# Attention outputs of four chunks in one visit of TensorE, with the state term in 32x32 tiles

## The chip, the cores and the metric

The kernel runs on one core of one Trainium2 chip. The metric is the device time of one execution, in microseconds (us). The core has TensorE (PE, with its weight loads shown apart as PEld), VectorE (DVE), ScalarE (ACT), GpSimd (POOL) and SyncE (SP), whose queue issues nearly all transfers (DMAs) here.

## What is computed

Two blocks, one after the other. The first is a Mamba-2 attention over 4 sequences of 768 tokens with 8 heads, head size 32 and state size 16. In the kernel's chunks of 128 tokens (the reference cuts into chunks of 32, which is the same sum) it reads, for each sequence and head:

```python
cum = np.cumsum(log_a_of_chunk, axis=-1)
M = (C @ B.T) * causal * np.exp(cum[:, None] - cum[None, :])
y = M @ x + (C @ state) * np.exp(cum)[:, None]          # inner term + state term
state = exp(cum[-1]) * state + (B * exp(cum[-1] - cum)[:, None]).T @ x
```

The second takes the 3072 tokens (256 columns, 8 heads of 32) through four expert networks, all of them for every token, weighted by the token's normalised probabilities:

```python
for e in range(4):
    out += p[:, e:e+1] * (np.maximum(x @ w1[e], 0) @ w2[e])   # w1 256x1024, w2 1024x256
```

All data is fp32.

## The kernel before

**Chunks and blocks.** There are 24 chunks of 128 tokens; chunk c belongs to sequence c % 4, so chunks c and c + 4 follow each other in one sequence, and the state that chunk c leaves is read by chunk c + 4. The chunks form five blocks for the expert networks, of 4, 4, 4, 6 and 6 chunks (`Block`, L302). Blocks of four use a Strassen-like scheme of 2x2 products, blocks of six one of 3x3 (L273 to L299). The weights are cut into 16 pieces of 256 columns (`fb`). A unit (L1257 to L1267) is the work of a block on some of these pieces: the first layer of this unit is put between the second layer of the unit before (`put`, L1222).

**The engines' parts.** PE does all products (`product`, L826, matmul at L830: 128x128 weights, 256 columns). ACT copies banks of PSUM to SBUF (`snap`, L839; `visit`, L1085) and back (`seed`, L844). DVE and POOL combine (L857), gate (L865), and add up weights (L919) and results (L1136). SP's queue loads weights (L418, L424, L895), sums of weights stored before (L916, stored at L924), gates (L818) and tokens.

**Attention for a pair of chunks.** While a block runs, the next block's chunks are worked in pairs: `fetch` (L700) loads tokens (`load_tokens`, L391: x, B, and B and C transposed), decays for rows (`load_heads`, L404) and decays for columns (L401). `decays` (L714) makes the decay matrix LT by scans on DVE (L455), the masked C (ctm, L436 on ACT), the decay of the state term (dec, L735 on DVE) and cts = ctm x dec (L738 on POOL). `scores` (L742) is one visit of PE for a pair: C B^T by heads in row tiles of 32x128 (L443) into four banks, which DVE multiplies by LT into MT (`masked`, L600). `outputs` (L759) is another visit for the pair: the state term (L774), then the inner term (`inner`, L468, four column tiles of 128x32 at a time), each chunk into a bank of its own. ACT copies the bank to yT (L790), and its last 16 columns by heads, the new state, to A (`keep_state`, L473). `carry` (L797) makes the state S on DVE: a transpose (L806), the decayed old state added (L808), and M = S spread over 4 column groups with zeros elsewhere (L811 with `qmask`, L524).

**The state term before.** A 128-row operand of C holds 8 heads of 16 state rows, two heads to each 32 rows. The state term runs as two matmuls of 64x64 a chunk; in each, M's zeros keep the two groups of 32 rows apart. In chunks 4 and up with odd number, the rows are held with their halves exchanged (`turned_round`, L346), so that a pair uses all four 64x64 tiles of the array. For that their tokens are loaded in three pieces (L394 to L396) and their decays in two (L407, L408), and the state is kept in two copies (L475, L476).

**What sets the order.** PE's order is a list (`line`) written by the loops from L1257 on. `PAIRS_AT` (L33) tells in which unit of a block which pair of the next block is worked; the score visit stands at place `SC` = 1 of the unit's list and the output visit at place `OUT` = 14 (L1330 to L1345). All other engines are ordered by a planner (`Plan`, L61): each work has a cost in us, the latest time at which PE can do with it (`times`), and buffers out of pools (`homes`, L368: 33 V, 32 W, 8 banks, 4 xb, 2 MT, 2 ctm, 2 cts, ...); the planner walks through time, gives each engine the most urgent work that is ready, and so writes the queues once, when the program is built. On the chip each queue runs in that order. In the built program, each transfer of SP also waits for the landing of the one eight issues before it.

Of the kernel before, what the change touches and what calls it, by code (L numbers as in the profile page):

```python
# [12 lines left out]
P = 128  # L13
# [7 lines left out]
KEEP = 5  # L21
NV, NW = 33, 32
SC, OUT = 1, 14
SLACK, BACK, YIELD = 0.0, 1.0, 6.0
# [3 lines left out]
RATE, MARGIN = 310.0, 4.0  # L28
AFTER = 1
HELD = ("x", "w"), (5, 8), (0, 7)  # L30
LAST = (0, 1), (0, 2), (1, 1), (1, 2), (0, 0), (1, 0)
LATE = (13, 2), (6, 9), (11, 4), (10, 12), (3,), (1, 14), ("x", "w"), (5, 8), (0, 7)
PAIRS_AT = {(3, 2): {0: 0, 1: 1}, (4, 2): {0: 0, 2: 1}, (4, 3): {0: 0, 1: 1, 2: 2},  # L33
            (6, 3): {0: 0, 2: 1, 3: 2}}

# [25 lines left out]
class Plan:  # L61
# [12 lines left out]
    def add(self, on, fn, reads=(), writes=(), part=(), lag=0.0, due=None, reuse=None, two=False,  # L74
            port=True, after=None, kb=0):
        w = Work(on, fn, lag)
        w.two, w.port, w.after, w.kb = two, port, after, kb
# [85 lines left out]
    def run(self, line, at, begin):  # L163
# [18 lines left out]
        while todo:  # L182
            e = min(t, key=lambda e: t[e])
            now = t[e]
            best, soon = None, None
            late = self.late = max(0.0, t["PE"] - line[head].nominal) if head < len(line) else 0.0
            for w in waiting[e]:
# [121 lines left out]
def kernel(  # L309
# [35 lines left out]

    def turned_round(c):  # L346
        return c >= NSEQ and c % 2 == 1

# [16 lines left out]
    def some(n, shape, name, pool=const):  # L365
# [9 lines left out]
        "LT": some(2, [P, NH, P], "LT"),  # L375
        "MT": some(2, [P, NH, P + N], "MT"),
        "ctm": some(2, [HN, NT, P], "ctm"),
        "cts": some(2, [HN, NT, P], "cts"),
        "dec": some(4, [HN, P], "dec"),
        "A": some(4, [P, NT, N], "A"),  # L380
        "S": some(6, [HN, D], "S"),
        "M": some(6, [HN, NQ, D], "M"),
        "gate": some(3, [P, max(b.n for b in blocks), P], "gate"),
# [7 lines left out]
    def load_tokens(c, xb):  # L391
        src = xbc[real(c)]
        if turned_round(c):
            nc.sync.dma_start(out=xb[:, :OBT], in_=src[:, :OBT])  # L394
            nc.sync.dma_start(out=xb[:HALF, OBT:], in_=src[HALF:, OBT:])
            nc.sync.dma_start(out=xb[HALF:, OBT:], in_=src[:HALF, OBT:])  # L396
        else:
            nc.sync.dma_start(out=xb, in_=src)
# [5 lines left out]
    def load_heads(c, ah):  # L404
        src = ac_d[real(c)].unsqueeze(1).to_broadcast([NH, N, P])
        if turned_round(c):
            nc.sync.dma_start(out=ah[:HALF], in_=src[NH // 2:])  # L407
            nc.sync.dma_start(out=ah[HALF:], in_=src[:NH // 2])  # L408
        else:
            nc.sync.dma_start(out=ah, in_=src)  # L410

# [37 lines left out]
    def quarter(c, r):  # L449
        q = r ^ 2 * turned_round(c)  # L450
        return slice(NT * q, NT * q + NT)
# [21 lines left out]
    def keep_state(c, A, y):  # L473
        if c % 2:
            nc.scalar.copy(out=A[:HALF], in_=y[HALF:])  # L475
            nc.scalar.copy(out=A[HALF:], in_=y[:HALF])  # L476
        else:
            nc.scalar.copy(out=A, in_=y)

# [43 lines left out]
    nc.vector.memset(zeros, 0.0)  # L523
    qmask = const.tile([P, NQ, D], FP32)  # L524
    nc.vector.memset(qmask, 0.0)
    for q in range(NQ):
        nc.vector.memset(qmask[32 * q:32 * q + 32, q], 1.0)
    own = const.tile([P, 1], FP32)
# [159 lines left out]

    yT, gates, S, M = {}, {}, {}, {}
    yT[0, 0] = plan.taken("V", NV - 3, now)  # L690
# [9 lines left out]
    def fetch(c):  # L700
        s = st[c]
        if "xb" not in s:
            s["xb"] = value("xb")
            dma(lambda e: load_tokens(c, s["xb"].t), 3 if turned_round(c) else 1, 320,
                part=[s["xb"]])
        if c >= NSEQ:
            s["ah"] = value("ah")
            dma(lambda e: load_heads(c, s["ah"].t), 2 if turned_round(c) else 1, 64,
                part=[s["ah"]])
# [32 lines left out]
    def scores(cs):  # L742
# [5 lines left out]
        for r in (3, 2, 0, 1):  # L748
            for j, c in enumerate(cs):
                s = st[c]  # L750
                dve(.42, lambda e, c=c, r=r, s=s, j=j: masked(
                    c, r, s["MT"].t, s["LT"].t, gs_[r].t, j), reads=[gs_[r], s["LT"]],
                    part=[s["MT"]])

# [4 lines left out]
    def outputs(cs):  # L759
# [4 lines left out]
        reads = [st[c][k] for c in cs for k in ("xb", "MT", "cts") if k in st[c]]  # L764
        reads += [M[c - NSEQ] for c in cs if c >= NSEQ]

        def fn(e):
            vs = {}
            for c in cs:
                vs[c] = v = ys[c].t[:, :NT * (P + N)].rearrange("p (t s) -> p t s", t=NT)  # L770
                for h in range(2) if c >= NSEQ else ():
                    rows = slice(HALF * h, HALF * h + HALF)
                    to = HALF * (1 - h if turned_round(c) else h)
                    nc.tensor.matmul(  # L774
                        out=v[to:to + HALF, :, 0:P],
                        lhsT=M[c - NSEQ].t.rearrange("p q d -> p (q d)")[rows, rows],
                        rhs=st[c]["cts"].t[rows], start=True, stop=False,
                        tile_position=(HALF * h, to), skip_group_check=True)
            for c in cs:
# [3 lines left out]

        pe((.96 if cs[0] >= NSEQ else .75) * len(cs), fn, reads=reads, writes=list(ys.values()))
        for c in cs:
# [6 lines left out]
            if c < NCH - NSEQ:  # L792
                s["A"] = value("A")
                act(.34 if c % 2 else .18, lambda e, c=c, s=s, y=y: keep_state(
                    c, s["A"].t, v(y)[:, :, P:]), reads=[y], part=[s["A"]])

    def carry(c):  # L797
        s = st[c]
        if "A" not in s:
            return  # L800
        S[c], M[c] = value("S"), value("M")
        more = [S[c - NSEQ], s["dec"]] if c >= NSEQ else []

        def fn(e):
            t = S[c].t
            nc.vector.transpose(t, s["A"].t.rearrange("p t n -> p (t n)"))  # L806
            if more:
                nc.vector.scalar_tensor_tensor(  # L808
                    out=t, in0=more[0].t, scalar=more[1].t[:, P - 1:P], in1=t,
                    op0=ALU.mult, op1=ALU.add)  # L810
            nc.vector.tensor_mul(M[c].t, t.unsqueeze(1).to_broadcast([HN, NQ, D]), qmask)  # L811

        dve(.82 if more else .54, fn, two=True, reads=[s["A"], *more], writes=[S[c], M[c]])

# [475 lines left out]
    for u, (k, groups) in enumerate(units):  # L1290
# [38 lines left out]
        if k < len(blocks) - 1:  # L1329
            p = PAIRS_AT[len(of_block), blocks[k + 1].scheme.pairs].get(i)  # L1330
            if p is not None:
                cs = [blocks[k + 1].first + 2 * p + j for j in range(2)]
                for c in cs:
                    fetch(c)
                    decays(c)
                for x, make in ((SC, scores), (OUT, outputs)):
                    mark = len(line)
                    make(cs)
                    at[x] = line[mark:]
                    del line[mark:]  # L1340
                for c in cs:
                    carry(c)
        for x, w in enumerate(merged):
# [56 lines left out]
```

## Time and profile before

| | us |
|---|---|
| median of three runs | 630.37 (629.18 to 632.73) |
| the execution that was profiled | 630.59 |
| its span | 628.8 |
| PE busy / weight loads | 622.6 / 529.3 |
| DVE busy | 526.0 |
| ACT busy | 261.9 |
| POOL busy | 254.3 |
| big matmuls, L830, 2656 records | first at 12.8, last visits of attention at 418 |

A record is half of an fp32 matmul: the hardware runs each as two passes, and the trace shows both. In a line of the view in order of time stand the start, the time from the first start to the last end, engine, line, operation, output and inputs, sizes (rows and columns of the tile, then the moving operand), and the number of records; in brackets the idle time ahead of it and who ended it. In a line of a group stand the busy time, the mean of one in ns, and the idle time ahead. "PEq", "SPq" and the like are the engines' queues. Ends of matmuls are modelled; their starts are used here.

### The profile page before, as it was taken

The numbers are of one execution on the slowest core, as the hardware profiler recorded it, in microseconds if no ns is written. First come the engines' busy times: TensorE is split into PE (matmuls) and PEld (weight loads), VectorE is DVE, ScalarE is ACT, GpSimd is POOL, SyncE is SP. The second block draws the span as 40 slices with busy tenths as digits, with TensorE's granted clock in tenths as the row PEclk, the third lists the DMA queues.
The fourth block names the chain that finished last, engine by engine and source line by source line (L and its number), as shares of the span: only waits on it lengthen the run. The fifth ranks groups of instructions, "written<-read, shape, count | busy, mean of one in ns | idle before, by whom it ended". The sixth has DMA issues, their size and how long they took to land.

```text
span 628.8 us, 10190 instructions
## 1 busy us (share of the span) xinstructions
PE 622.6 (99%) x3363; PEld 529.3 (84%) x3363; DVE 526.0 (84%) x869; ACT 261.9 (42%) x538; POOL 254.3 (40%) x267
## 2 busy tenths in 40 slices
PE   9999999999999999999999999999999999999997
PEld 5787888888888888878888888888888888888886
DVE  7988899899997699988778988978787977768684
ACT  4222642434434353344433336355444235455441
POOL 4153552625534764543666421414045521233130
PEclk9999999999999999999999999999999999999999
DMA  7999795484898965699997827546123333951001
GB/s 206 307 304 346 231 302 197 123 282 126 287 336 298 315 189 164 173 322 334 349 365 244 280 63 250 176 118 199 57 80 94 101 73 80 361 176 47 1 1 51
DMA packets 110932, 125.87 MB, mean 200 GB/s; under 512 B 28692, under 2 KB 76832, under 8 KB 110880
## 3 DMA queue, kind: packets, MB, share of 16 engines
q1 hardware_dynamic: 110500, 124.97, 62.3%
q8 instruction: 27, 0.44, 0.3%
q10 hardware_dynamic: 380, 0.25, 0.1%
q14 instruction: 25, 0.20, 0.1%
HBM read 100.30 MB, written 24.89 MB: 199 GB/s over the span
## 4 chain that ended last, share of the span: by engine, by line
PE 93%; DMA 3%; DVE 2%; ACT 1%; issue 0%; SPq 0%; POOL 0%; ACTq 0%; POOLq 0%; DVEq 0%
PE bank L830 87%; PE bank L468 2%; DMA ab<-acut_d 2%; PE bank L443 2%; DMA w<-in_w_dram 1%; PE bank L774 1%; PE bank L603 1%; PE bank L580 0%; DVE LT L455 0%; DVE v L857 0%; DVE v L865 0%; POOL v L857 0%; DVE MT L600 0%; SPq L418 0%; DVE w L919 0%
## 5 line engine op out<-in xcount | busy, mean ns | idle before, releaser
L830 PE MATMUL bank<-v,w 128*128 128x256 f32 x1864 | 438.9, 380 | 0.0
L830 PEld LDWEIGHTS bank<-v,w 128*128 128x128 f32 x1864 | 352.1, 190 | 53.6 <-issue 4.0
L830 PE MATMUL bank<-Y,w 128*128 128x256 f32 x792 | 203.1, 379 | 1.2 <-ACT v L839 1.2
L857 POOL TENSOR_TENSOR v<-v,v 128x512 f32<-128x512 f32 x71 | 101.0, 1424 | 190.4 <-DVE v L857 84.4
L857 DVE TENSOR_TENSOR v<-v,v 128x512 f32<-128x512 f32 x199 | 162.8, 841 | 17.9 <-ACT v L839 14.5
L830 PEld LDWEIGHTS bank<-Y,w 128*128 128x128 f32 x792 | 150.1, 190 | 22.7 <-ACT v L839 2.0
L865 DVE SCALAR_TENSOR_TENSOR v<-bank,gate 128x512 f32<-128x512 f32 x172 | 116.7, 686 | 41.5 <-PE bank L830 34.2
L1085 ACT COPY v<-bank 128x512 f32<-128x512 f32 x107 | 62.6, 585 | 163.3 <-PE bank L830 161.9
L844 ACT COPY bank<-v 128x512 f32<-128x512 f32 (+1 forms) x192 | 108.1, 578 | 27.3 <-DVE v L857 24.4
L919 POOL TENSOR_TENSOR w<-w,w 128x256 f32<-128x256 f32 x102 | 89.9, 901 | 40.3 <-PE bank L830 29.6
L839 ACT COPY v<-bank 128x512 f32<-128x512 f32 x106 | 61.9, 585 | 100.7 <-PE bank L830 97.7
L455 DVE TENSOR_TENSOR_SCAN LT<-ab,ident 128x512 f32<-128x512 f32 x42 | 54.1, 1306 | 2.6 <-DMA ab<-acut_d 2.6
L857 DVE TENSOR_TENSOR v<-bank,v 128x512 f32<-128x512 f32 x40 | 27.6, 689 | 17.6 <-PE bank L830 16.4
L738 POOL TENSOR_TENSOR cts<-ctm,dec 128x256 f32<-128x256 f32 x20 | 19.1, 965 | 43.5 <-DVE dec L735 20.8
L1136 POOL TENSOR_TENSOR v<-v,v 128x256 f32<-128x256 f32 x20 | 17.1, 865 | 45.2 <-ACT v L1085 45.1
L600 DVE TENSOR_TENSOR MT<-bank,LT 128x256 f32<-128x256 f32 x93 | 32.1, 414 | 0.3
L436 ACT ACTIVATE ctm<-xb,tmask 128x128 f32<-128x128 f32 x48 | 15.9, 392 | 27.8 <-DMA w<-in_w_dram 9.8
L1136 DVE TENSOR_TENSOR v<-v,v 128x256 f32<-128x256 f32 x40 | 18.6, 493 | 4.6 <-ACT v L1085 4.3
L461 POOL TENSOR_TENSOR MT<-xb,LT 128x128 f32<-128x128 f32 x20 | 11.1, 566 | 21.9 <-DVE LT L455 20.7
L919 DVE TENSOR_TENSOR w<-w,w 128x256 f32<-128x256 f32 x36 | 17.4, 506 | 0.2
L990 DVE TENSOR_TENSOR bank<-bank,v 128x512 f32<-128x512 f32 x22 | 15.2, 691 | 2.6 <-PE bank L830 2.6
L919 POOL TENSOR_TENSOR w<-w 128x256 f32<-128x256 f32 x13 | 10.2, 790 | 17.4 <-DMA w<-in_w_dram 15.8
(76 smaller groups left out, 216.3 us busy)
## 6 DMA issues: line engine op xcount, KB each, us to landing
w<-in_w_dram SPq DMA_DIRECT2D x130, 256.0 KB
w<-w_d SPq DMA_DIRECT2D x130, 256.0 KB
w_d<-w SPq DMA_DIRECT2D x82, 256.0 KB
ab<-acut_d SPq DMA_DIRECT2D x21, 512.0 KB
w<-in_w_dram SPq DMA_DIRECT2D x38, 128.0 KB
xb<-in_xbc_dram SPq DMA_DIRECT2D x12, 320.0 KB
gate<-p_d SPq DMA_DIRECT2D x10, 384.0 KB
gate<-p_d SPq DMA_DIRECT2D x11, 256.0 KB
```

The lines of the kernel that those rows point to most:

```text
L436: nc.scalar.mul(ctm[:, t], xb[:, OCT:OCT + P], tmask[:, t:t + 1])
L455: nc.vector.tensor_tensor_scan(out=LT.rearrange("p h s -> p (h s)")[:, lo:lo + w], data0=src, data1=ident.rearrange("p h s -> p (h s)")[:, ...
L600: nc.vector.tensor_mul(MT[:, h, 0:P], g, LT[:, h])
L738: plan.add({"POOL": .78}, lambda e: nc.gpsimd.tensor_mul(s["cts"].t, s["ctm"].t, s["dec"].t.unsqueeze(1).to_broadcast([HN, NT, P])), reads ...
L830: nc.tensor.matmul(out=o, lhsT=w[:, j], rhs=x if half is None else x[:, j], start=(start and j == 0), stop=(j == 1), skip_group_check=True)
L839: act(.6, lambda e: nc.scalar.copy(out=flat(v), in_=bank.t), reads=[bank], writes=[v])
L844: act(.6 if to > FB else .38, lambda e: nc.scalar.copy(out=bank.t[:, :to], in_=flat(v)[:, :to]), reads=[v], writes=[bank])
L857: plan.add(engines, lambda e: (on(e).tensor_add if sign > 0 else on(e).tensor_sub)(flat(v), whole(x), whole(y)), reads=[x, y], writes=[v], ...
L865: dve(.7 if x.kind == "bank" else .74, lambda e: nc.vector.scalar_tensor_tensor(out=h.t, in0=whole(x).rearrange("p (j m) -> p j m", j=JJ), ...
L919: plan.add({"POOL": .78} if due else B256, lambda e, r=r, x=x, y=y, sign=sign: (on(e).tensor_add if sign > 0 else on(e).tensor_sub)(view(r ...
L1085: act(.6, lambda e: nc.scalar.copy(out=flat(v), in_=bank.t), reads=[bank], writes=[v])
L1136: plan.add(engines, lambda e: (on(e).tensor_add if sign > 0 else on(e).tensor_sub)(o[1](), x[1](), y[1]()), reads=[v for v in vs if v is n ...
```

## The change

1. `outputs` may take four chunks in one visit. `PAIRS_AT` now lists, for each unit, place and work: `s0` is the scores of pair 0, `o01` the outputs of pairs 0 and 1. Blocks 1 and 2 (four chunks) have `o01` in the place of the second pair's outputs, block 3 (six chunks) has `o0` and `o12`, block 4 has three single pairs.
2. The state term is four matmuls of 32x32 a chunk, straight from S. M, `qmask` and the multiply at L811 are gone. The rows of heads are permuted by `turn_of(c)`, (0, 2, 1, 3) by c % 4: group r of 32 rows writes to rows of group r XOR turn, so four chunks use all 16 tiles.
3. For that, tokens and decays of a chunk are loaded, and its state kept, in 1, 2 or 4 pieces (`pieces_of`): with turn 0, 2 and 1 or 3.
4. Buffers: 31 V and 28 W (were 33 and 32); 4 MT, ctm and cts (were 2), 8 dec (4), 10 S (6), and no M (6).
5. The planner: `masked` works aim at 8 us ahead of PE's need (`HOLD`), and DVE may wait up to 0.3 us for a work that is more urgent by 1.0 us or more (`NEAR`, `WORTH`).

```diff
+    def turn_of(c):
+        return (0, 2, 1, 3)[c % NSEQ]
+
+    def pieces_of(c):
+        x = turn_of(c) if c >= NSEQ else 0
+        n = {0: P, 2: HALF}.get(x, P // NQ)
+        return [(i * n ^ x * (P // NQ), i * n, n) for i in range(P // n)]
...
+PAIRS_AT = {
+    (3, 2): ((0, 1, "s0"), (1, 1, "s1"), (1, 14, "o01")),
+    (4, 2): ((0, 1, "s0"), (2, 1, "s1"), (2, 14, "o01")),
+    (4, 3): ((0, 1, "s0"), (0, 14, "o0"), (1, 1, "s1"), (2, 1, "s2"), (2, 14, "o12")),
+    (6, 3): ((0, 1, "s0"), (0, 14, "o0"), (2, 1, "s1"), (2, 14, "o1"), (3, 1, "s2"), (3, 14, "o2")),
+}
...
     def load_tokens(c, xb):
-        if turned_round(c):
+        if len(pieces_of(c)) > 1:
             nc.sync.dma_start(out=xb[:, :OBT], in_=src[:, :OBT])
-            nc.sync.dma_start(out=xb[:HALF, OBT:], in_=src[HALF:, OBT:])
-            nc.sync.dma_start(out=xb[HALF:, OBT:], in_=src[:HALF, OBT:])
+            for there, here, n in pieces_of(c):
+                nc.sync.dma_start(out=xb[here:here + n, OBT:], in_=src[there:there + n, OBT:])
...
     def load_heads(c, ah):
+        for there, here, n in pieces_of(c):
+            nc.sync.dma_start(out=ah[here:here + n], in_=src[there // N:(there + n) // N])
...
     def keep_state(c, A, y):
+        for there, here, n in pieces_of(c % NSEQ + NSEQ):
+            nc.scalar.copy(out=A[here:here + n], in_=y[there:there + n])
...
     def outputs(cs):
-                for h in range(2) if c >= NSEQ else ():
-                    rows = slice(HALF * h, HALF * h + HALF)
-                    to = HALF * (1 - h if turned_round(c) else h)
+                for r in range(NQ) if c >= NSEQ else ():
+                    rows, to = slice(32 * r, 32 * r + 32), 32 * (r ^ turn_of(c))
                     nc.tensor.matmul(
-                        out=v[to:to + HALF, :, 0:P],
-                        lhsT=M[c - NSEQ].t.rearrange("p q d -> p (q d)")[rows, rows],
+                        out=v[to:to + 32, :, 0:P], lhsT=S[c - NSEQ].t[rows],
                         rhs=st[c]["cts"].t[rows], start=True, stop=False,
-                        tile_position=(HALF * h, to), skip_group_check=True)
+                        tile_position=(32 * r, to), skip_group_check=True)
-        pe((.96 if cs[0] >= NSEQ else .75) * len(cs), fn, reads=reads, writes=list(ys.values()))
+        pe(.93 + .49 * len(cs) if cs[0] >= NSEQ else .75 * len(cs), fn, reads=reads, writes=list(ys.values()))
...
     def carry(c):
-            nc.vector.tensor_mul(M[c].t, t.unsqueeze(1).to_broadcast([HN, NQ, D]), qmask)
...
     def times(self, line, at):
+            if w.hold:
+                last += [n.nominal + w.hold for n in w.needs if "PE" in n.on]
...
     def run(self, line, at, begin):
-                elif soon is None or when < soon:
-                    soon = when
+                else:
+                    if e == "DVE" and when <= now + NEAR and (near is None or rank < near[0]):
+                        near = rank, when
+                    if soon is None or when < soon:
+                        soon = when
+            if best and near and near[0] < best[0] - WORTH:
+                best, soon = None, near[1]
```

More of the change, by code (lines that the diff above doesn't have):

```diff
@@ L21 @@
 KEEP = 5
-NV, NW = 33, 32
-SC, OUT = 1, 14
+NV, NW = 31, 28
 SLACK, BACK, YIELD = 0.0, 1.0, 6.0
@@ L29 @@
 AFTER = 1
+HOLD = 8.0
+NEAR, WORTH = .3, 1.0
 HELD = ("x", "w"), (5, 8), (0, 7)
@@ L32 @@
 LATE = (13, 2), (6, 9), (11, 4), (10, 12), (3,), (1, 14), ("x", "w"), (5, 8), (0, 7)
-PAIRS_AT = {(3, 2): {0: 0, 1: 1}, (4, 2): {0: 0, 2: 1}, (4, 3): {0: 0, 1: 1, 2: 2},
-            (6, 3): {0: 0, 2: 1, 3: 2}}
+PAIRS_AT = {
[4 rows of a table added]
+}
 class Home:
@@ L74, in add @@
     def add(self, on, fn, reads=(), writes=(), part=(), lag=0.0, due=None, reuse=None, two=False,
-            port=True, after=None, kb=0):
+            port=True, after=None, kb=0, hold=0.0):
         w = Work(on, fn, lag)
+        w.hold = hold
         w.two, w.port, w.after, w.kb = two, port, after, kb
@@ L184, in run @@
             now = t[e]
-            best, soon = None, None
+            best, soon, near = None, None, None
             late = self.late = max(0.0, t["PE"] - line[head].nominal) if head < len(line) else 0.0
@@ L344, in real @@
         return c % NSEQ * NC + c // NSEQ
-    def turned_round(c):
-        return c >= NSEQ and c % 2 == 1
+    def turn_of(c):
[4 more added lines that the diff above has]
+        return [(i * n ^ x * (P // NQ), i * n, n) for i in range(P // n)]
     const = ctx.enter_context(tc.tile_pool(name="const", bufs=1))
@@ L375 @@
         "LT": some(2, [P, NH, P], "LT"),
[L376 to L379, printed above, removed]
+        "MT": some(4, [P, NH, P + N], "MT"),
+        "ctm": some(4, [HN, NT, P], "ctm"),
+        "cts": some(4, [HN, NT, P], "cts"),
+        "dec": some(8, [HN, P], "dec"),
         "A": some(4, [P, NT, N], "A"),
-        "S": some(6, [HN, D], "S"),
-        "M": some(6, [HN, NQ, D], "M"),
+        "S": some(10, [HN, D], "S"),
         "gate": some(3, [P, max(b.n for b in blocks), P], "gate"),
@@ L405, in load_heads @@
         src = ac_d[real(c)].unsqueeze(1).to_broadcast([NH, N, P])
[L406 to L410, printed above, removed]
+        for there, here, n in pieces_of(c):
+            nc.sync.dma_start(out=ah[here:here + n], in_=src[there // N:(there + n) // N])
     def w1_rows(fb, k):
@@ L449, in quarter @@
     def quarter(c, r):
-        q = r ^ 2 * turned_round(c)
+        q = r ^ (turn_of(c) if c >= NSEQ else 0)
         return slice(NT * q, NT * q + NT)
@@ L473, in keep_state @@
     def keep_state(c, A, y):
[L474 to L478, printed above, removed]
+        for there, here, n in pieces_of(c % NSEQ + NSEQ):
+            nc.scalar.copy(out=A[here:here + n], in_=y[there:there + n])
     aq0 = homes["V"][-1][:, 0].rearrange("p (t s) -> p t s", t=NT)
@@ L523 @@
     nc.vector.memset(zeros, 0.0)
[L524 to L527, printed above, removed]
     own = const.tile([P, 1], FP32)
@@ L685, in value @@
         return Value(kind, **kw)
-    yT, gates, S, M = {}, {}, {}, {}
+    yT, gates, S = {}, {}, {}
     yT[0, 0] = plan.taken("V", NV - 3, now)
@@ L703, in fetch @@
             s["xb"] = value("xb")
-            dma(lambda e: load_tokens(c, s["xb"].t), 3 if turned_round(c) else 1, 320,
+            dma(lambda e: load_tokens(c, s["xb"].t), len(pieces_of(c)) + (len(pieces_of(c)) > 1), 320,
                 part=[s["xb"]])
@@ L707, in fetch @@
             s["ah"] = value("ah")
-            dma(lambda e: load_heads(c, s["ah"].t), 2 if turned_round(c) else 1, 64,
+            dma(lambda e: load_heads(c, s["ah"].t), len(pieces_of(c)), 64,
                 part=[s["ah"]])
@@ L752, in scores @@
                     c, r, s["MT"].t, s["LT"].t, gs_[r].t, j), reads=[gs_[r], s["LT"]],
-                    part=[s["MT"]])
+                    part=[s["MT"]], hold=HOLD)
     def pair_of(c):
@@ L764, in outputs @@
         reads = [st[c][k] for c in cs for k in ("xb", "MT", "cts") if k in st[c]]
-        reads += [M[c - NSEQ] for c in cs if c >= NSEQ]
+        reads += [S[c - NSEQ] for c in cs if c >= NSEQ]
         def fn(e):
@@ L793, in outputs @@
                 s["A"] = value("A")
-                act(.34 if c % 2 else .18, lambda e, c=c, s=s, y=y: keep_state(
+                act(.17 * len(pieces_of(c % NSEQ + NSEQ)), lambda e, c=c, s=s, y=y: keep_state(
                     c, s["A"].t, v(y)[:, :, P:]), reads=[y], part=[s["A"]])
@@ L800, in carry @@
             return
-        S[c], M[c] = value("S"), value("M")
+        S[c] = value("S")
         more = [S[c - NSEQ], s["dec"]] if c >= NSEQ else []
@@ L810, in fn @@
                     op0=ALU.mult, op1=ALU.add)
-            nc.vector.tensor_mul(M[c].t, t.unsqueeze(1).to_broadcast([HN, NQ, D]), qmask)
-        dve(.82 if more else .54, fn, two=True, reads=[s["A"], *more], writes=[S[c], M[c]])
+        dve(.54 if more else .27, fn, two=True, reads=[s["A"], *more], writes=[S[c]])
     def load_gate(k, e):
@@ L1329 @@
         if k < len(blocks) - 1:
[L1330 to L1342, printed above, removed]
+            for unit, x, what in PAIRS_AT[len(of_block), blocks[k + 1].scheme.pairs]:
+                if unit != i:
+                    continue
+                cs = [blocks[k + 1].first + 2 * int(p) + j for p in what[1:] for j in range(2)]
+                mark = len(line)
+                if what[0] == "s":
+                    for c in cs:
+                        fetch(c)
+                        decays(c)
+                    scores(cs)
+                else:
+                    outputs(cs)
+                    for c in cs:
+                        carry(c)
+                at[x] = line[mark:]
+                del line[mark:]
         for x, w in enumerate(merged):
```

## The prediction

> **What bounds the kernel now.** I read the page first, then the groups by shape, then single stretches in order of time, and last the waits.
>
> ```profile
> span 628.8 us, 10190 instructions
> PE 622.6 (99%) x3363; PEld 529.3 (84%) x3363; DVE 526.0 (84%) x869; ACT 261.9 (42%) x538; POOL 254.3 (40%) x267
> ...
> PE 93%; DMA 3%; DVE 2%; ACT 1%; issue 0%; SPq 0%; POOL 0%; ACTq 0%; POOLq 0%; DVEq 0%
> ```
>
> PE never stops, and it makes up 93% of the chain that ended last. So a change pays by what it takes out of PE's queue, plus what it takes from PE's few stalls. DVE at 84% matters only where PE then waits for it. The execution profiled took 630.59 us, 1.8 of them around the span of 628.8; the median of the runs shown is 630.37, 0.2 less.
>
> One visit of attention outputs (a pair of chunks), PE in order of time:
>
> ```profile
> 50.27 1.24 PE L830 MATMUL bank<-Y,w 128*128 128x256 f32 x5
> 51.44 0.66 PE L774 MATMUL bank<-cts,M 64*64 64x256 f32 x8
> 52.03 1.19 PE L468 MATMUL bank<-MT,xb 128*32 128x144 f32 x32
> 53.15 1.13 PE L830 MATMUL bank<-v,w 128*128 128x256 f32 x4
> 54.12 1.67 PE L830 MATMUL bank<-Y,w 128*128 128x256 f32 x7
> ```
>
> Big matmuls (L830) start 0.216 us apart in the trace's records, so the last one before the visit starts at 50.27 + 4 x 0.216 = 51.13 and the next at 53.15: 2.02 us instead of 0.216. The four that follow take 54.12 - 53.15 = 0.97 instead of 0.86, another 0.10. A visit costs PE 2.02 - 0.22 + 0.10 = 1.91 us. Its parts: entry 0.31 (51.13 to 51.44), state term 0.59, inner term and exit 1.12. The single records show the inner term as eight steps of four matmuls, 0.1225 us each: 0.98, and 0.14 for the exit. Only the steps scale with the chunks; entry, exit and restart are fixed.
>
> PE has only two stalls over 0.2 us between the first visits and the tail: 0.69 us at 41.7 and 0.81 at 274.9, both with one form:
>
> ```profile
> 269.81 0.58 SPq L396 DMA_DIRECT2D xb<-in_xbc_dram x1
> ...
> 274.71 0.69 ACT L436 ACTIVATE ctm<-xb,tmask 128x128 f32<-128x128 f32 x2 [4.64 <-POOL v L857]
> ...
> 275.31 0.56 ACT L839 COPY v<-bank 128x512 f32<-128x512 f32 x1
> ...
> 275.93 1.13 PE L830 MATMUL bank<-Y,w 128*128 128x256 f32 x4 [0.65 <-ACT v L839]
> ```
>
> ```profile
> 41.40 0.69 ACT L436 ACTIVATE ctm<-xb,tmask 128x128 f32<-128x128 f32 x2 [1.72 <-DMA xb<-in_xbc_dram]
> 42.00 1.05 ACT L839 COPY v<-bank 128x512 f32<-128x512 f32 x2
> ```
>
> A chunk's tokens land late, the mask (L436) that needs them holds ACT's queue, and the bank copy behind it (L839) comes late for PE. POOL, named at 274.71, feeds nothing to that mask; its last token piece was issued 4.9 us earlier. So ACT's order and SP's queue, not their load, are where this kernel is hurt. What the change touches on DVE and SP:
>
> ```profile
> L811 DVE TENSOR_TENSOR M<-S,qmask 128x128 f32<-128x128 f32 x20 | 6.8, 338 | 0.7
> ```
>
> ```profile
> L398 SPq DMA_DIRECT2D xb<-in_xbc_dram x12: 341/448/797, 5.5 to 342.2; - x12
> L394 SPq DMA_DIRECT2D xb<-in_xbc_dram x10: 328/333/488, 15.2 to 336.8; - x10
> L395 SPq DMA_DIRECT2D xb<-in_xbc_dram x10: 483/520/536, 16.9 to 337.2; - x10
> L396 SPq DMA_DIRECT2D xb<-in_xbc_dram x10: 466/568/1799, 17.7 to 337.7; - x10
> ```
>
> A piece costs SP about as much to issue as a whole chunk: 0.52 to 0.57 against 0.45 us (min/median/max in ns).
>
> [...] 0.31 us at the entry of a visit, and four tiles of 64x64 that start 7 ns apart. [...] a chunk's two row tiles write one bank, and their second passes still begin 0.27 us after the first[...]. [...] four row tiles (L443) and four column tiles (L468) each run side by side in this trace.
>
> **The change, part by part.**
>
> *Merged visits.* By the table of units, the outputs of blocks 1 and 2 (four chunks each) and of the last four chunks of block 3 come in one visit: six pair visits become three. The other four stay pairs, and every score visit (L443) stays. A merged visit has entry 0.31, 16 inner steps 16 x 0.1225 = 1.96, exit 0.14, and a state term of 16 tiles. Tile starts are 7 ns apart, so 12 more tiles add 0.08 to the 0.59; narrower weights may give back 0.03; I take 0.65. Gap: 0.31 + 0.65 + 1.96 + 0.14 = 3.06; cost 3.06 - 0.22 + 0.10 = 2.94. Two pair visits cost 3.82. Gain 0.88 each, **2.6 us** for three, all on PE's own path. Bounds: the state term can't fall under 0.59 (gain 0.94 each, 2.8); if the 16 tiles run in two rounds of two passes of 0.24, 0.48 comes on top (gain 0.40 each, 1.2); in four rounds 1.45 (a loss of 0.57 each).
>
> *32x32 in the pair visits.* 8 tiles for 4: four more starts, 0.03, against the narrower weights, 0.03: nothing, or up to 0.48 each (1.9 for four) if they don't overlap.
>
> *M goes.* 20 multiplies of 0.338 = 6.8 us of DVE, and five memsets at the start. In the steady part this is cover, not path: PE waits for DVE nowhere there by more than 0.2 us. At the start the output visit at 17.0 us begins 0.22 us late; an earlier DVE may win that. Taken at nothing. Some of the room goes back: the new order puts 12 operand sums more on POOL (0.8 to 0.9 us each) and so many fewer on DVE (0.5).
>
> *Copies of state by pieces.* 1, 2, 4, 4 copies for four chunks instead of 1, 2, 1, 2: 25 more of 0.18 = 4.5 us of ACT, which is 42% busy. They sit behind the copies of yT (0.37) of the same visit. Cover: ACT's idle time; uncovered, one copy ahead of a bank copy costs up to 0.18. A merged visit leaves 4 x 0.37 + 11 x 0.18 = 3.5 us for ACT at once. I put 0.1 on each of the three, 0.3.
>
> *Loads by pieces.* Per four chunks xb takes 1, 3, 5, 5 issues (was 1, 3, 1, 3) and ah 1, 2, 4, 4 (was 1, 2, 1, 2): 55 more over five rounds, at 0.55 to 0.6 us with the gap 30 to 33 us of SP, in some 400 us in which SP issues a third to four fifths of the time. The bytes stay. Behind them in SP's queue stand the loads of w, ab and gates. And SP lets each transfer wait for the landing of the one eight issues before it, so small pieces take slots from large ones. Cover: the lead of each load. In the order of the new program, PE work between the visit that frees a token buffer and the bank copy behind the mask comes to 14.5 to 17.5 us for most chunks (15 to 19 for the short ones before, over 38 for the others). Five pieces 2.9, landing 5.5 (early ones took 5 to 6), mask and copy 1.3: 9.7. That leaves 5 us for SP's lag. Without it the stall is as above, 0.7 to 0.8 each.
>
> *Fewer buffers.* V 33 to 31, W 32 to 28 pay for the doubled MT, ctm, cts and dec. A w tile is now freed at least 21 us of PE work ahead of the next product from it, 30 before; against 5.5 of landing and SP's lag that still hides.
>
> *Moved.* Where visits merge, the first pair's yT copies, A copies and carry come one or two units (20 to 75 us) later. Their readers, the next block's token sums and the outputs a block on, already wait for the second pair. Taken at nothing; if late, a token sum is 0.42 to 0.57 per step.
>
> *The stalls.* The one at 274.9 follows a burst of 16 output transfers straight ahead of the token loads; in the new order some 30 issues stand between such bursts and the next token loads: gone, 0.8. The one at 41.7 hangs on chunk 7: five more issues ahead of its last piece but nearly the same bytes; I give it 0.5 of its 0.7. Together -1.3. DVE's order is closer in block 1 (a score bank is freed without room to spare): +0.1.
>
> Sum: 630.59 - 2.6 - 1.3 + 0.3 + 0.1 = 627.1; 0.2 less for the median: **626.9 us**.
>
> **The rivals.**
>
> *Given back in small stalls* (0.23): DVE's and ACT's orders are packed anew and some ten places lose 0.1 to 0.2 each, or both old stalls remain. For: with W and V cut, the order has less room. Against: so few stalls before. 626.9 + 1.6 = 628.5, from 627.6 to 629.8.
>
> *Tokens late* (0.11), slower: where SP runs over 5 us behind, mask, bank copy and PE stall 0.8 us as at 274.9. SP was 6 to 9 us behind its releases there. If it happens on 8 of the 16 chunks loaded after the first: 626.9 + 6.4 = 633.3. It outweighs the gain from five such chunks on.
>
> *Tiles in turn* (0.06), slower: 32x32 tiles that write one bank run one after the other[...]: three merged visits lose 0.57 instead of gaining 0.88 (4.4 worse), the four pairs 0.48 each (1.9): 626.9 + 6.3 = 633.2.
>
> **How the numbers follow.** Forecast case 0.60, from 625.7 (both stalls gone, 2.8 from the visits, nothing lost) to 627.9. A measurement of this kernel tells about 0.5% from no change, 3.15 us: under 627.2 is faster. Three quarters of the forecast case lie there, 0.46; the rest and most of the first rival, 0.38, are within; the two last rivals, with little unforeseen beside them, 0.16 slower. Range 625.5 to 630.3: it leaves out most of the slower cases.
>
> **What would show it.** Merged visits: from the last big matmul before to the first after, 3.06 us, 16 inner steps of 0.1225, a state term of 0.65. If the state term is over 1.0, tiles go in turn. The pair visits stay at 2.02. No L839 copy in late position behind an L436 mask at 275; if token loads are late, PE's idle time names ACT and ACT's mask a DMA of xb. DVE's busy time falls by some 10 us without PE noticing. It is wrong if PE's stalls between visits add up to over 2 us.

## The result, and the profile after

| | before | after |
|---|---|---|
| median of four runs each, us | 629.97 (629.18 to 632.73) | 638.38 (637.51 to 642.45) |
| ratio of after to before | | 1.0135 [1.0089, 1.0181] |
| the execution that was profiled: time, span | 630.59, 628.8 | 642.45, 640.6 |
| transfers issued by SP, time spent on issuing | 651, 284.9 | 706, 314.9 |

The change made the kernel 1.35% slower. It was forecast at 626.9, with a range up to 630.3: wrong in sign and outside the range. The profiled execution is the slowest of the four, some 4 us over their median, so it shows more loss than a usual one; what it has beyond the others is taken up under "Why the prediction was wrong".

The page of the kernel after: span, busy time, granted clock, the chain's shares by engine, and the group of the scans that make the decay matrix. In the trace of after, lines stand 6 to 16 further down than before: L836 is the big matmul, L782 the state term, L484 the inner term, L459 the scores, L452 the mask, L845 the copy of a bank to SBUF, L871 the gate, L471 the scan for LT, L744 the decay of the state term; L413 and L415 load tokens, L426 decays for rows, L420 decays for columns. The kernels of the experiments shift them again. The last line here is the scans' group before.

```profile
span 640.6 us, 10430 instructions
PE 626.7 (98%) x3443; PEld 532.2 (83%) x3443; DVE 509.9 (80%) x833; ACT 267.5 (42%) x563; POOL 254.7 (40%) x278
...
PEclk9999899999999999998999999999999999999999
...
PE 86%; DMA 7%; DVE 4%; SPq 2%; issue 1%; DVEq 0%; ACT 0%
...
L471 DVE TENSOR_TENSOR_SCAN LT<-ab,ident 128x512 f32<-128x512 f32 x42 | 53.4, 1287 | 18.5 <-DMA ab<-acut_d 18.5
```

```profile
L455 DVE TENSOR_TENSOR_SCAN LT<-ab,ident 128x512 f32<-128x512 f32 x42 | 54.1, 1306 | 2.6 <-DMA ab<-acut_d 2.6
```

PE's share of the chain fell from 93% to 86%, and DMA's rose from 3% to 7%. DVE has 16 us less to do (526.0 before), and gains nothing by it: its scans now stand idle for 18.5 us for the decays for columns (ab), where it was 2.6 before. PEclk, the clock that TensorE was granted, in tenths for each fortieth of the span, drops in two slices: its record has it at half from 61.55 to 68.38 us and from 293.66 to 297.07.

**What the change was made for happened as forecast.** A merged visit, PE in order of time:

```profile
79.53 1.03 PE L836 MATMUL bank<-Y,w 128*128 128x256 f32 x4
80.48 0.71 PE L782 MATMUL bank<-cts,S 32*32 32x256 f32 x32
81.13 2.18 PE L484 MATMUL bank<-MT,xb 128*32 128x144 f32 x64
83.24 1.13 PE L836 MATMUL bank<-v,w 128*128 128x256 f32 x4
84.21 0.59 PE L836 MATMUL bank<-Y,w 128*128 128x256 f32 x2
```

The single records put the last big matmul before it at 80.175 and the first after it at 83.242: 3.07 us, forecast 3.06. The state term takes 81.13 - 80.48 = 0.65, and the restart still 0.97 for four. The visit at 182.4 takes 3.07 too, and the pair visits at 237.0 and 346.9 stay at 2.02.

**What was lost are stalls of PE that were not there.** From the starts of PE's records:

| at, us | lost, us | what came late |
|---|---|---|
| 42.2 (and 45.6) | 2.42 (0.17) | tokens (xb) of chunk 7 |
| 58.8 (and 62.3) | 3.23 (0.34) | decays for columns (ab) |
| 62.8 to 67.1 | 2.1 | nothing: the clock is at half, and ten records of L836 are 0.427 us apart instead of 0.216 |
| 67.1, a score visit | 0.58 | nothing: still at half clock |
| 220.8 (and 226.7, 229.6) | 1.08 (0.21, 0.47) | decays for rows (ah) |
| 289.8, in a merged visit | 2.77 | decays for columns (ab) |
| the same visit, inner term | 1.66 | nothing: the clock is at half |

Together 15.0 us. Less 2.6 for three merged visits and 1.5 for the two old stalls, one of which (274.9) is gone and the other of which is the first row here, this is 10.9 of the 11.8 by which the span grew; 0.5 more lies in a later start (the first big matmul at 13.25 for 12.78).

The stall at 42.2, SP's queue, ACT and PE in order of time:

```profile
37.17 2.64 SPq L426 DMA_DIRECT2D ah<-ac_d  x4
39.92 0.35 SPq L413 DMA_DIRECT2D xb<-in_xbc_dram  x1
40.37 1.77 SPq L415 DMA_DIRECT2D xb<-in_xbc_dram  x4
...
43.64 0.69 ACT L452 ACTIVATE ctm<-xb,tmask 128x128 f32<-128x128 f32 x2 [5.89 <-DMA xb<-in_xbc_dram]
44.24 0.56 ACT L845 COPY v<-bank 128x512 f32<-128x512 f32 x1
...
44.85 2.27 PE L836 MATMUL bank<-Y,w 128*128 128x256 f32 x8 [2.25 <-ACT v L845]
```

This is the chain that the forecast showed at 41.7: late tokens, the mask, the copy behind it on ACT, PE. Only it is three times as long. Four pieces of decays and five of tokens are issued one after the other from 37.17 to 42.14; before, the decays were one or two issues.

The stall at 58.8, the same view:

```profile
47.56 0.40 SPq L420 DMA_DIRECT2D ab<-acut_d  x1
...
50.54 0.81 SPq L420 DMA_DIRECT2D ab<-acut_d  x1
...
54.03 1.23 DVE L471 TENSOR_TENSOR_SCAN LT<-ab,ident 128x512 f32<-128x512 f32 x1 [7.53 <-DMA ab<-acut_d]
...
61.47 0.66 DVE L871 SCALAR_TENSOR_TENSOR v<-bank,gate 128x512 f32<-128x512 f32 x1
...
62.28 5.46 PE L836 MATMUL bank<-v,w 128*128 128x256 f32 x12 [3.07 <-DVE v L871]
```

DVE runs in a fixed order, so it stands for 7.53 us at a scan whose ab is not there; the gates (L871) behind the scans come late, and a gate is what frees a bank of PSUM for PE. PE names the gate, but the gate was only held up by the scan, and the scan by SP. The last line also shows the clock: 12 records in 5.46 us, where a full clock does four in 1.03.

The merged visit that took 7.50 us, the same view:

```profile
285.42 0.40 SPq L420 DMA_DIRECT2D ab<-acut_d  x1
...
291.15 1.23 DVE L471 TENSOR_TENSOR_SCAN LT<-ab,ident 128x512 f32<-128x512 f32 x1 [3.58 <-DMA ab<-acut_d]
...
292.29 0.67 DVE L871 SCALAR_TENSOR_TENSOR v<-bank,gate 128x512 f32<-128x512 f32 x1
...
293.01 0.63 PE L782 MATMUL bank<-cts,S 32*32 32x256 f32 x8 [2.17 <-DVE v L871]
293.57 3.84 PE L484 MATMUL bank<-MT,xb 128*32 128x144 f32 x64
```

Again ab, the scan, the gate: here the bank that it frees is one of the four that the visit writes, and PE stops with three of four chunks' state terms done. The last line adds the clock: the inner term's 64 records take 3.84 us, where at 81.13 they took 2.18.

### The profile page after: what moved, and what is told of

It reads as the page before. It is cut to its first block, busy times and chain, and to the rows that moved or that the text cites. A ratio compares the mean times of both kernels' runs of the same rounds, so it can differ in the third digit from the quotient of the medians.

```text
span 640.6 us, 10430 instructions
## 1 busy us (share of the span) xinstructions
PE 626.7 (98%) x3443; PEld 532.2 (83%) x3443; DVE 509.9 (80%) x833; ACT 267.5 (42%) x563; POOL 254.7 (40%) x278
## 4 chain that ended last, share of the span: by engine, by line
PE 86%; DMA 7%; DVE 4%; SPq 2%; issue 1%; DVEq 0%; ACT 0%
PE bank L836 81%; DMA ab<-acut_d 3%; PE bank L484 2%; PE bank L459 1%; DMA w_d<-w 1%; DMA acut_d<-a_cut 1%; DMA w<-in_w_dram 1%; DVE MT L609 1%; DMA ah<-ac_d 1%; DVE LT L471 1%; DVE v L863 1%; PE bank L612 1%; DVE v L871 1%; PE bank L782 1%; SPq L930 0%
## 5 line engine op out<-in xcount | busy, mean ns | idle before, releaser
L836 PE MATMUL bank<-v,w 128*128 128x256 f32 x1864 | 442.0, 382 | 4.3 <-DVE v L871 4.0
L836 PEld LDWEIGHTS bank<-v,w 128*128 128x128 f32 x1864 | 353.7, 191 | 59.4 <-POOL MT L477 3.4
L836 PE MATMUL bank<-Y,w 128*128 128x256 f32 x792 | 203.3, 380 | 2.3 <-ACT v L845 2.3
L863 POOL TENSOR_TENSOR v<-v,v 128x512 f32<-128x512 f32 x72 | 99.1, 1384 | 181.3 <-DVE v L863 72.1
L836 PEld LDWEIGHTS bank<-Y,w 128*128 128x128 f32 x792 | 150.1, 190 | 23.8 <-ACT v L845 3.1
L863 DVE TENSOR_TENSOR v<-v,v 128x512 f32<-128x512 f32 x198 | 156.0, 812 | 16.9 <-ACT v L845 13.5
L871 DVE SCALAR_TENSOR_TENSOR v<-bank,gate 128x512 f32<-128x512 f32 x172 | 116.2, 684 | 44.4 <-PE bank L836 36.3
L925 POOL TENSOR_TENSOR w<-w,w 128x256 f32<-128x256 f32 x112 | 96.5, 880 | 98.6 <-PE bank L836 41.4
L845 ACT COPY v<-bank 128x512 f32<-128x512 f32 x106 | 62.1, 586 | 113.4 <-PE bank L836 110.6
L471 DVE TENSOR_TENSOR_SCAN LT<-ab,ident 128x512 f32<-128x512 f32 x42 | 53.4, 1287 | 18.5 <-DMA ab<-acut_d 18.5
L863 DVE TENSOR_TENSOR v<-bank,v 128x512 f32<-128x512 f32 x40 | 27.6, 689 | 19.6 <-PE bank L836 16.4
L1142 POOL TENSOR_TENSOR v<-v,v 128x256 f32<-128x256 f32 x18 | 15.2, 853 | 38.2 <-ACT v L1091 32.5
L1142 DVE TENSOR_TENSOR v<-v,v 128x256 f32<-128x256 f32 x42 | 23.1, 581 | 2.7 <-ACT v L1091 2.5
L452 ACT ACTIVATE ctm<-xb,tmask 128x128 f32<-128x128 f32 x48 | 16.5, 395 | 17.2 <-DMA xb<-in_xbc_dram 17.0
L996 DVE TENSOR_TENSOR bank<-bank,v 128x512 f32<-128x512 f32 x22 | 15.2, 691 | 3.0 <-PE bank L836 3.0
L925 POOL TENSOR_TENSOR w<-w 128x256 f32<-128x256 f32 x15 | 12.7, 846 | 10.2 <-PE bank L836 5.2
L747 POOL TENSOR_TENSOR cts<-ctm,dec 128x256 f32<-128x256 f32 x20 | 15.2, 774 | 3.6 <-DVE dec L744 3.0
L484 PEld LDWEIGHTS bank<-MT,xb 128*32 128x32 f32 x384 | 12.5, 119 | 4.9 <-issue 3.7
```

Source lines behind the costliest of these rows:

```text
L452: nc.scalar.mul(ctm[:, t], xb[:, OCT:OCT + P], tmask[:, t:t + 1])
L471: nc.vector.tensor_tensor_scan(out=LT.rearrange("p h s -> p (h s)")[:, lo:lo + w], data0=src, data1=ident.rearrange("p h s -> p (h s)")[:, ...
L484: nc.tensor.matmul(out=y[32 * q:32 * q + 32, 0:w], lhsT=xb[:, h * D:h * D + D], rhs=MT[:, NT * q + t, 0:w], start=start, stop=True, tile_p ...
L836: nc.tensor.matmul(out=o, lhsT=w[:, j], rhs=x if half is None else x[:, j], start=(start and j == 0), stop=(j == 1), skip_group_check=True)
L845: act(.6, lambda e: nc.scalar.copy(out=flat(v), in_=bank.t), reads=[bank], writes=[v])
L863: plan.add(engines, lambda e: (on(e).tensor_add if sign > 0 else on(e).tensor_sub)(flat(v), whole(x), whole(y)), reads=[x, y], writes=[v], ...
```

## The experiments

Two theories. **Issues**: 55 more transfers in SP's queue make everything behind them late. **Order**: the new order, with merged visits that hold four banks and with fewer buffers, is too tight for the loads it has, and the pieces only make that visible. A third is that it is the transfers themselves, many small ones, that slow the rest down.

Several runs load a chunk's tokens or decays in one issue although the rows of heads are permuted. The permutation is made where the arrays are laid out for the kernel, next to the transposes that are done there already: in sequence b, from the second chunk on, the groups of 32 rows change places in those arrays (B and C, transposed or not, and the decays) for which the run needs it, and the kernel's indices of heads (`quarter`, `inner`) follow. The results and the bytes stay.

### Loads whole, in the order of after: tokens alone, tokens and decays

```diff
-        if len(pieces_of(c)) > 1:
-            nc.sync.dma_start(out=xb[:, :OBT], in_=src[:, :OBT])
-            for there, here, n in pieces_of(c):
-                nc.sync.dma_start(out=xb[here:here + n, OBT:], in_=src[there:there + n, OBT:])
+        nc.sync.dma_start(out=xb, in_=src)            # both
...
-        for there, here, n in pieces_of(c):
-            nc.sync.dma_start(out=ah[here:here + n], in_=src[there // N:(there + n) // N])
+        nc.sync.dma_start(out=ah, in_=src)            # the second only
...
+    def turned(v):
+        for b, x in enumerate((0, 2, 1, 3)):
+            k = slice(b * NC + 1, b * NC + NC)
+            v[k] = v[k][:, :, [q ^ x for q in range(NQ)]]
```

> The changed kernel in its own order, with the tokens of a chunk loaded by one transfer: the permuted rows come from the layout of the input. The decays stay in pieces, so 40 of SP's 75 extra small issues go (tokens took 1, 3, 5, 5 issues and now 1). Loads in pieces as the cause: the stalls at 42 us (2.4) and part of those at 59 and 290 go, 630 to 634 us. Fewer V and W buffers, or the new order and its rules, as the cause: 636 to 639, as the changed kernel.

> The changed kernel in its own order, with tokens and decays of every chunk loaded by one transfer each: all permuted rows come from the layout of the inputs. Loads in pieces as the cause: the stalls in front of and inside visits fall from about 13 us to under 3, the 2.7 us of the merged visits stay, 626 to 629. Fewer buffers or the new order as the cause: nothing that matters changes, 636 to 639.

The number of issues in the first text is wrong: tokens whole are 50 issues fewer than in after, decays whole 35 fewer, both 85.

The experiments ran in three batches, in which before took 631.59, 631.58 and 630.92 us (629.97 in the result's). So kernels of different batches are compared by their ratios to before, and their differences are given as per cent of before's time; 0.1% is 0.63 us. After is at 1.0135.

Measured: tokens whole 630.63, ratio to before 0.9989 [0.9973, 1.0005], with 656 issues; of the stalls, 0.47 at 61.4 and 1.15 in the last merged visit are left in the profiled execution, which at 628.71 is one of the faster of its 20. Both whole **626.94, ratio 0.9936 [0.9908, 0.9964]**, 621 issues. The page of the second:

```profile
span 624.7 us, 10309 instructions
PE 619.8 (99%) x3443; PEld 529.4 (85%) x3443; DVE 512.7 (82%) x833; ACT 267.5 (43%) x563; POOL 256.6 (41%) x278
...
PE 99%; DVE 1%; issue 0%; ACT 0%; DVEq 0%
...
L464 DVE TENSOR_TENSOR_SCAN LT<-ab,ident 128x512 f32<-128x512 f32 x42 | 53.8, 1295 | 1.9 <-DMA ab<-acut_d 1.7
```

DMA is gone from the chain, the scans wait 1.7 us for ab instead of 18.5, all three merged visits take 3.07, and PE has no stall over 0.2 us. The order is that of after, with its 31 V and 28 W and its four banks a visit. All engines' instructions stand in the same order as in after. So the order is not what is too tight: without the extra issues it is faster than before, and 1.99% of before's time (12.5 us) faster than with them. How SP falls behind is seen in the loads of ab, the same ones in the same order. Whole loads:

```profile
37.89 0.32 SPq L415 DMA_DIRECT2D ab<-acut_d  x1
...
40.72 0.92 SPq L415 DMA_DIRECT2D ab<-acut_d  x1
...
44.04 1.21 DVE L464 TENSOR_TENSOR_SCAN LT<-ab,ident 128x512 f32<-128x512 f32 x1
```

| load of ab | issued in after | loads whole | SP's issues ahead of it | time of these, us |
|---|---|---|---|---|
| second | 24.55 | 22.34 | 26 / 24 | 13.6 / 11.7 |
| third | 33.74 | 27.09 | 37 / 31 | 20.0 / 15.2 |
| fourth | 47.56 | 37.89 | 60 / 43 | 31.3 / 20.4 |
| fifth | 50.54 | 40.72 | 65 / 48 | 33.4 / 22.5 |

The fourth load of ab is 9.7 us late. The 17 issues more ahead of it account for 10.9 us of issuing; the time between issues is even 1.2 shorter (15.2 for 16.4). So SP is late by the time that it spends on issuing, not by waiting for landings.

### Empty issues

```diff
         nc.sync.dma_start(out=xb, in_=src)
+        n = len(pieces_of(c))
+        tiny(c, n + (n > 1) - 1)
...
         nc.sync.dma_start(out=ah, in_=src)
+        tiny(c, len(pieces_of(c)) - 1)
...
+    def tiny(c, n):
+        for _ in range(n):
+            i = next(slots)
+            nc.sync.dma_start(out=scrap[:, i:i + 1], in_=xbc[real(c)][:32, :1])
```

Loads whole, and in the place of the 85 issues that this saves, 85 transfers of 32 rows of 4 bytes into a tile that nobody reads.

> The run with tokens and decays loaded whole, in the same order, with as many tiny transfers (32 rows of 4 bytes, read by nobody) put behind each load as the changed kernel has pieces beyond the first: 85 in all. If the number of issues on SP's queue makes the loads late, whatever they carry: 634 to 640. If it is the bytes moved in short rows or the permutation itself: 627 to 628.

Measured: 635.99, ratio to before 1.0082 [1.0051, 1.0113]. The page, then SP's, DVE's and PE's lines in order of time:

```profile
span 635.2 us, 10393 instructions
...
PE 86%; DMA 7%; DVE 4%; issue 1%; SPq 1%; ACT 0%; ACTq 0%; DVEq 0%
...
L475 DVE TENSOR_TENSOR_SCAN LT<-ab,ident 128x512 f32<-128x512 f32 x42 | 52.9, 1274 | 15.7 <-DMA ab<-acut_d 15.7
```

```profile
46.18 0.39 SPq L425 DMA_DIRECT2D ab<-acut_d  x1
...
49.24 0.68 SPq L425 DMA_DIRECT2D ab<-acut_d  x1
...
52.20 1.22 DVE L475 TENSOR_TENSOR_SCAN LT<-ab,ident 128x512 f32<-128x512 f32 x1 [7.10 <-DMA ab<-acut_d]
...
60.44 4.25 PE L840 MATMUL bank<-v,w 128*128 128x256 f32 x12 [2.69 <-DVE v L875]
```

This is the profile of after again: the chain's shares, the scans' 15.7 us, the fourth and fifth ab at 46.18 and 49.24, the 7 us of DVE, the stall at 57.4 (2.85), one at 41.8 (1.41), and 2.5 us in the last merged visit. The transfers carry 11 KB in all, and nobody reads them. Of the 1.99% between after and loads whole, 1.46% come back (1.0082 - 0.9936; 9.2 of 12.5 us). The price of an issue, in the records of one line of each kernel (min/median/max in ns): a piece of decays in after, a whole load of decays, an empty issue:

```profile
L426 SPq DMA_DIRECT2D ah<-ac_d x55: 515/583/706, 37.2 to 288.6; - x55
```

```profile
L420 SPq DMA_DIRECT2D ah<-ac_d x20: 574/602/882, 31.8 to 273.2; - x20
```

```profile
L416 SPq DMA_DIRECT2D scrap<-in_xbc_dram x85: 310/419/1495, 17.6 to 350.6; - x85
```

A piece of 32 rows costs SP as much as the whole 128 rows; the empty ones are a quarter cheaper than a piece of decays, which fits that not all of the loss comes back. The third theory, that the many small transfers slow the others, this run alone doesn't exclude, for its empty ones are small transfers too. The time from issue to use does: the fourth ab is issued at 47.56 and its scan starts at 54.03 in after, 6.5 us; with empty issues it is 46.18 and 52.20, 6.0. Before, the scans that waited for an ab started 5.6 us (21.91 to 27.51) and 5.8 us (28.67 to 34.51) after its issue. So an ab that comes up to 9.7 us late was issued late; on its way it loses under 1 us.

### Decays alone whole

The edit of `load_heads` above, without that of `load_tokens`: 35 issues fewer than after.

> The changed kernel in its own order, with the decays of a chunk loaded by one transfer (35 issues fewer over all chunks) and the tokens still in pieces. If every small issue counts alike: 60% of the loss stays, 632 to 635. If the tokens' pieces alone make the stalls: 636 to 639. If the decays' pieces were the greater part: under 631.

Measured: 631.03, ratio 0.9994 [0.9981, 1.0007]; it lies just over the last range of the text and in none. The stall at 41.2 (2.67 us) stays, since chunk 7's tokens are still in pieces; those at 58.8, 220.8 and 289.8 are gone. So each half of the pieces, taken away alone, wins back 1.4 to 1.5% of the 1.99 (about 9 of 12.5 us). They do not add up. This fits a stall that comes only where SP's lag passes what the buffers cover, so that either half taken away keeps the lag under that in most places; it was not shown apart.

### The order of before, with the loads cut as in after, and with whole loads

```diff
+    def cut(c):
+        n = (P, HALF, 32, 32)[c % NSEQ]
+        return [((i * n + HALF * turned_round(c)) % P, i * n, n) for i in range(P // n)]
...
-            nc.sync.dma_start(out=xb[:HALF, OBT:], in_=src[HALF:, OBT:])
-            nc.sync.dma_start(out=xb[HALF:, OBT:], in_=src[:HALF, OBT:])
+            for there, here, n in cut(c):
+                nc.sync.dma_start(out=xb[here:here + n, OBT:], in_=src[there:there + n, OBT:])
```

> The kernel before in its own order, with loads cut as the changed kernel cuts them (tokens 1, 3, 5, 5 issues and decays 1, 2, 4, 4 per four chunks). Loads in pieces as the cause: its token and decay loads come later, stalls at 41.7 and 274.9 grow and others join, 633 to 638. Otherwise: within 1 us of before, 630.

> The kernel before in its own order, with its exchanged halves put into the layout of the inputs, so that every chunk's tokens and decays come by one transfer each. Loads in pieces as the cause of late loads: the stalls at 41.7 and 274.9 (1.5 us) go or shrink, 628.5 to 630. If those stalls come from the order of ACT alone: 630 to 631.

The loads of decays are cut in the same way. Measured: before with after's number of issues (706), 638.69, ratio 1.0110 [1.0077, 1.0143], somewhat over the range of the text; before with whole loads (the arrays permuted by the turns 0, 2, 0, 2), 629.14, ratio 0.9964 [0.9952, 0.9977]. The first has the stall at 42.3 just as after has it:

```profile
39.92 2.10 SPq L400 DMA_DIRECT2D xb<-in_xbc_dram  x4
...
43.42 0.69 ACT L437 ACTIVATE ctm<-xb,tmask 128x128 f32<-128x128 f32 x2 [3.55 <-DMA xb<-in_xbc_dram]
...
44.02 1.05 ACT L840 COPY v<-bank 128x512 f32<-128x512 f32 x2
...
44.63 2.84 PE L831 MATMUL bank<-Y,w 128*128 128x256 f32 x8 [1.98 <-ACT v L840]
```

Pieces alone, in the old order and with nothing else of the change, cost 7.1 us (638.69 - 631.59, before in the same batch), most of what after loses. And the 1.5 us of old stalls were of the same kind: with whole loads both are gone. So before, too, had 0.36% to gain by whole loads.

### Buffers, merged visits

```diff
-NV, NW = 33, 32
+NV, NW = 31, 28
```

> The kernel before with 31 V and 28 W buffers in place of 33 and 32, planned anew. Fewer buffers as the cause: loads start later and DVE waits for weights, 634 to 638. Loads in pieces as the cause: within 2 us of before, 629 to 632.

Measured, before with fewer buffers: 630.44, ratio 0.9991 [0.9977, 1.0006]. They cost nothing that can be told.

```diff
-    (4, 2): ((0, 1, "s0"), (2, 1, "s1"), (2, 14, "o01")),
+    (4, 2): ((0, 1, "s0"), (0, 14, "o0"), (2, 1, "s1"), (2, 14, "o1")),
```

The same for the other two places with merged visits; loads whole, state term in 32x32 tiles.

> As the run with tokens and decays loaded whole, but with every output visit for one pair of chunks, planned anew. If a merged visit is worth 0.9 us of PE, as the trace of the changed kernel says, three pairs of visits cost 2.7 us more: 629 to 630.5. If the gain of that run came from the whole loads alone, 627.

Measured: 629.57, ratio 0.9973 [0.9955, 0.9990], against 0.9936 with merged visits. The trace shows why: six pair visits of 2.02 instead of three of 3.07, with the restarts 2.6 us; its two stalls (0.75 at 275.9, 0.58 in a score visit for 0.12) add 1.2, and its start is 0.4 sooner: 3.4, where the spans differ by 3.3. The two intervals overlap slightly, so the 2.6 rests on PE's records, not on the medians.

### Can the order hide the pieces?

The planner reckons 0.38 us of SP for each issue. Two runs plan again: after, with 0.62 us for each piece; and loads whole, with one issue counted for each load.

```diff
-        return plan.add({"SP": .38 * n}, ...)
+        return plan.add({"SP": .62 * n if n > 1 and kb in (64, 320) else .38 * n}, ...)
```

> The changed kernel with all its pieces, but the planner counts 0.62 us of SP for each piece in place of 0.38, and orders the queues anew. If the loss is a wrong price in the planner: loads are issued earlier, 628 to 632. If SP's time and its eight transfers in flight are the limit whatever the order: 634 to 639.

> The run with tokens and decays loaded whole, and the planner told so (one issue each), so that all queues are ordered anew. PE has no stall left to lose in the run before: 626 to 627.5. If the new order brings stalls of its own: 628 and more.

Measured: the first 632.71, ratio 1.0019 [1.0005, 1.0034], between the two ranges of its text; the profiled execution, the fastest of its 20, has stalls of 2.12 at 55.2, 0.91 and 0.43. With the price nearer to what it is, over half of the loss goes (1.16% of 1.99) though all 706 issues stay. The second 628.60, ratio 0.9961 [0.9945, 0.9976]: more room made the order no better, it has 0.50 at 164.6 and 1.45 at 271.6 that the order of after doesn't have with the same loads. A new order can thus cost some 0.25% (1.6 us) by itself, though the intervals overlap; how much of the first run's gain is the price and how much such scatter is not shown.

## Why the prediction was wrong

**The step that failed** is "Loads by pieces", and in it the sentence "That leaves 5 us for SP's lag", on which 30 to 33 us of SP were taken at nothing. Their size was right (314.9 - 284.9 = 30.0 of issuing). The cover was not. It was worked out for the tokens alone, and the queue was described right beside it: "Behind them in SP's queue stand the loads of w, ab and gates." For ab and ah no lead was worked out. SP issued the fourth ab 9.7 us later than with whole loads; a DVE that waits at a scan takes the gates behind it along, and so PE's banks. Three of the four places in the table where something came late are ab and ah, not tokens. The prediction's own sign of being wrong came with them: stalls between visits that add up to over 2 us.

**The stall at 41.7** was given 0.5 of its 0.7 back, because of "five more issues ahead of its last piece but nearly the same bytes". The bytes are nearly the same in all these kernels, and the stall follows the issues: in after it is 2.42, with the old order and pieces 2.14, with whole loads nothing, and with whole loads and empty issues 1.41 again. The other old stall went as forecast.

**The rival "Tokens late"** had the right engine and the right sign, and 0.11. It named the tokens, at eight chunks of 0.8 us each; what came were few stalls of 1 to 3 us, most of them on decays, and half a clock after two of them. Its chance was small because the shares of SP's time ("a third to four fifths") were read as room, while in after, from 37 to 52 us, SP issues for 85% of the time and never pauses for more than 0.53 us.

**What held.** The large other terms of the sum. With the pieces taken away and everything else left, the profiled execution took 626.51, against 630.59 - 2.6 - 1.5 + 0.1 = 626.6 (merged visits, both old stalls, 0.12 in one score visit). That the median, 626.94, meets the forecast of 626.9 so closely is in part luck: before took 631.59 in that batch, not 630.37. Merged visits 3.07 for 3.06; pair visits 2.02, so 32x32 tiles in them are free; fewer buffers nothing; and no gain is seen from DVE's 16 us less, M's multiply among them. The 0.3 for copies of state was not seen. **The rival "Tiles in turn"** falls: 16 tiles take 0.65 where four took 0.59. Each chunk's bank is written by four row tiles (each to 32 partitions of its own), and all 16 tiles start within 0.10 us, their second passes 0.24 us after the first. In before, too, the four row tiles of a score visit and the four column tiles of an inner step start 7 ns apart. The 0.03 for narrower weights, an estimate, has its like in the weight loads: one takes 130 ns for 64x64 in before and 102 for 32x32 in after (medians).

Why the profiled execution of after lost some 4 us more than the others no trace shows in detail, but the recorded clocks say most of it: its mean is 0.990, theirs are 0.997 to 0.999. In its trace the clock is at half for 10.2 us between PE's first product and its last, at a cost of 4.7 us (2.1, 0.58 and 1.66 in the table, and the 0.34 at 62.3). A mean of 0.997 over 636 us leaves room for about 3.8 us at half clock. So the others lost, by this estimate, 3 to 4.7 us less to the clock.

What stays open: issuing the pieces from another engine's queue was not tried. Nor did a run show what pieces cost or bring where the DMA engines are mostly idle: in the kernel before they are 0.79 busy from 60 to 320 us, and there splitting cost 1.10%, through the one queue that issues everything.

The best version of those run is after with whole loads: 0.64% faster than before, by ratio 0.9936 [0.9908, 0.9964]. Whole loads alone give before 0.36% (0.9964 [0.9952, 0.9977]), so about 0.28% of it belong to the change itself; the intervals overlap, and PE's records of the visits (2.6 us) are the firmer ground for it.

## What to carry to other kernels

Count what a change adds to a DMA queue in issues, not in bytes, and follow everything behind them in that queue to its first reader: here 85 issues of nothing cost 9 us, through loads that the change had not touched. A queue that is busy half of the time on average (314.9 of 640.6 us here) has little room in a stretch where it issues almost without a break; take the lead of the load that is last to be issued there. If data must be permuted for a better layout on the array, permute it where it is laid out, not by cutting its load. Here the arrays are laid out before the kernel starts, so the permutation is outside the measured time; where it is not, it has its own cost.

## What the runs showed of the hardware

A stall of PE can cost about as much again after it has ended, because the granted clock may be halved. In the trace of after, the stall at 58.8 took 3.23 us and ended at 62.28; the clock is recorded at half from 61.55 to 68.38 us. Ten records were 0.427 us apart there instead of 0.216 (a factor of 1.98), and all the work at half clock cost 3.0 us. In the merged visit at 289.8 PE stood for 2.33 us until 293.01; the clock is recorded at half from 293.66 to 297.07, and the inner term cost 1.66 us more.

Not every such stall is followed by a half clock. These are all stalls of over 2 us in the traces of this case:

| stall | length, us | clock halved around its end | measured |
|---|---|---|---|
| after, 58.8 | 3.23 | yes | recorded at half for 6.83 us, from 61.55 |
| empty issues, 57.4 | 2.85 | yes | 12 records take 4.25 us at 60.44, where four take 1.03 at full clock |
| decays whole, 41.2 | 2.67 | yes | mean clock of this execution 0.997 |
| after, 42.2 | 2.42 | no | recorded at full from 6.94 to 61.55 |
| after, 290.5 (in the merged visit) | 2.33 | yes | recorded at half for 3.41 us, from 293.66 |
| before in pieces, 42.3 | 2.14 | yes | 8 records take 2.84 us at 44.63; in after, at full clock, 2.27 at 44.85 |
| planner told, 55.2 | 2.12 | no | mean clock of this execution 1.000 |
| empty issues, 286.6 | 2.08 | no | 9 tenths or more in its slice of PEclk |

The length does not tell the two kinds apart: 2.14 us was followed by a half clock and 2.42 was not. What decides it is not settled by these eight cases. So, in this kernel, a new stall of over 2 us is to be priced at up to 3 us more than its length (the 3.0 measured after the one at 58.8), an estimate from these traces.
